# A share of the first score tiles transposed by TensorE instead of by DMA, under a newly drawn order

## The chip, the cores and the metric

One core of a Trainium2 chip runs the whole program in one launch. The metric is the device time of that core in microseconds (us). The kernel before takes 526.13 us, the median of three runs (523.61 to 528.75).

## The reference

Three layers follow each other, for a batch of 2 and 768 positions, all in float32 accuracy.

1. Attention with 8 heads of 64: `scores = scale * q k^T`, and a score counts only where the hashes of query and key agree (the hash is the sign of six projections). Then `softmax(scores) @ v`.
2. A mixture of four experts over the 512 channels that come out. Each expert is a causal attention with its own projections `wq, wk, wv, wo`; a gate picks the best two experts of each position and weighs them.
3. A mix with the previous position (`mu * x + (1 - mu) * x_prev`), then `sigmoid(xr @ w_r) * (relu(xk @ w_k)^2 @ w_v)`. The weights `w_k, w_v, w_r` arrive as 64-bit floats.

## The kernel before, in words

**Accuracy by halves.** Matmuls take 16-bit operands, so each value is split into a high part and a low part (`hi_part`, `lo_part`), and three matmuls (high by high, high by low, low by high) stand for one.

**Units.** The 2 x 768 positions are cut into twelve units of 128 queries. Each unit goes through `lsh_steps` (the hashed attention, 8 heads), `moe_steps` (4 experts) and `mix_steps`. Units overlap: while unit 1 is in its heads, unit 0 is in its experts.

**One score tile** (`softmax`, line 746, and `split_p`, line 764). TensorE (PE) writes the scores of 128 queries against n keys into PSUM (tile `s`; `se` for an expert). VectorE (DVE) copies them to `P` and takes the row minimum (`mx`); a small DVE instruction scales that. ScalarE (ACT) takes the exponential in place and the row sum. The high part goes to the first half of tile `PHL`, by GpSimd (POOL) for two tiles in eight and by ACT for the others; the low part goes to its second half, by POOL. `turn` (line 538) then transposes `PHL` to `PT`, 2n/128 blocks of 128 x 128, and `pv` multiplies `PT` by the values. For a head n is 768, so that there are twelve blocks; for an expert n grows from 128 in the first unit of a batch to 768 in its sixth, and the tiles are called `P_m`, `PHL_m`, `PT_m`.

**The transpose.** `turn` has two ways. With `by_pe` 0 the SyncE queue (SP) issues one DMA transpose. Otherwise PE transposes the blocks into PSUM, and they are copied out: for more than eight blocks into two PSUM tiles with one copy each, by ACT where `by_pe` is 3. The first operands' transposes (`tr_y`, `tr_x`) take this way already, with copies by DVE. For score tiles line 768 chooses, by `NS[0]`, the number of the score tile in the order in which the program is built (heads and experts of unit 0, then of unit 1, and so on). It takes the PE way where n is 768, `NS[0]` is under `pn`, and `NS[0] * pp % 8 < pp`. With `pn=0` no score tile does.

**Buffers.** There are two PSUM tiles for scores and four others (tag `d`) that nearly everything else shares: the head sums `x`, the projections, the transposes, the decoding of the 64-bit weights. `P` has four buffers, `PHL` six, `PT` three.

**Weights.** `split_w` (the experts' weights) and `split_d` (the 64-bit weights, 20 tiles) load a tile from the ACT queue, decode it by ACT, POOL and DVE, and split it. That is done during the first units.

**The order.** `plan` (line 220) draws up the order of all instructions on every engine ahead of time. Each step has a due time (`times`, line 1095, in units; `L`, `M`, `X`, `wa`, `k1` and the like move them), less a lead for what is urgent (`ev` for the copy of the scores, `ex` for the exponential, `hs`, `hp`, `ht`). At each point every engine looks at its first `win` ready steps and takes the one that can start first; a step may be up to `wait` ns later and still be taken for its rank. Engines execute in that order, each strictly one after the other; they wait for each other by semaphores.

Of the kernel before, what the change touches and what calls it, by code (L numbers as in the profile page):

```python
# [13 lines left out]
AF = mybir.ActivationFunctionType  # L14
OP = mybir.AluOpType
# [408 lines left out]
def tile_lsh_moe_mix(  # L424
# [8 lines left out]
    nc = Program(tc.nc)  # L433
# [12 lines left out]
    HS = S // 2  # L446
    NP, NPHL, NPT = CONF["np"], CONF["nphl"], CONF["npt"]

# [9 lines left out]
    def ahead(what, f, *a):  # L458

        old, nc.ahead = nc.ahead, nc.ahead + (what,)  # L460
        r = f(*a)
        nc.ahead = old
        return r
# [21 lines left out]
    def DQ():  # L485
        return QS[CONF["dq"]]

    def LQ(i):
        return QS[CONF["lq"]] if i else nc.sync

    def OQ():
        return QS[CONF["oq"]]

# [82 lines left out]
    def split_w(src_dmas, shape, dst, sc, nm):  # L576
        w32 = sp.tile(shape, F32, tag="x2t", bufs=CONF["nx2"], name=f"w32_{nm}")
        for dap, sap in src_dmas:
            DQ().dma_start(dap(w32), sap)
        hi, lo = dst(0), dst(1)  # L580
        if CONF["wd"]:
            nc.gpsimd.tensor_scalar(w32, w32, sc, 1.0, op0=OP.mult, op1=OP.mult)
            hi_part("a", hi, w32)
            lo_part("p", lo, w32, hi)
        else:
            hi_part("p", hi, w32, sc)
            lo_part("v", lo, w32, hi, sc)
# [158 lines left out]
    def softmax(Sv, n, scale, sm, bias, nm, masked=None):  # L746


        Pt = sp.tile([P, S], F32, tag="P", bufs=NP, name=f"P_{nm}")[:, :n]
        PHL = sp.tile([P, 2 * S], F16, tag="PHL", bufs=NPHL, name=f"PHL_{nm}")[:, :2 * n]  # L750
        PT = sp.tile([P, 2 * NT, P], F16, tag="PT", bufs=NPT, name=f"PT_{nm}")[:, :2 * n // P]
        dst = Pt.rearrange("p (a s) -> p a s", a=2) if len(Sv.shape) == 3 else Pt
        if masked:
            def evict():
                nc.vector.tensor_scalar(dst, Sv, masked, None, op0=OP.min, op1=OP.min, accum_out=bias)
                nc.vector.tensor_scalar(bias, bias, scale, None, op0=OP.mult)
        else:
            def evict():
                nc.vector.tensor_scalar(dst, Sv, -scale, None, op0=OP.mult, op1=OP.min, accum_out=bias)
        ahead("ev", evict)  # L760
        ahead("ex", lambda: nc.scalar.activation(Pt, Pt, AF.Exp, bias=bias, scale=-scale if masked else -1.0, accum_out=sm))
        return ahead("ht", split_p, Pt, PHL, PT, n)
# [9 lines left out]
    NS = [0]  # L772
# [4 lines left out]
    def lsh_steps(i, LAG):  # L777
# [3 lines left out]
        def score(h):  # L781
            need(KS[b, h // G][:3] + QS_[i])
            if t0 == 0 and h % 2:
                need(KS[b, h // 4])
            if h == 0:
                st["sm"] = sp.tile([P, H], F32, tag="sm", name=f"sm_{i}")
                st["mx"] = sp.tile([P, H], F32, tag="mx", name=f"mx_{i}")
            kg = KG[b, h // G]
            hh = h % G
            Sp = ps_s.tile([P, 2, 512], F32, tag="s", name=f"s_{i}_{h}")  # L790
            for n in range(2):
                for a, (x, y) in enumerate((("x1", "y1"), ("x2", "y2"))):
                    nc.tensor.matmul(Sp[:, n, :HS], QX[i][x][:, h, :], kg[y][:, hh, n * HS:(n + 1) * HS],
                                     start=(a == 0), stop=(a == 1))
            st["pt"][h] = softmax(Sp[:, :, :HS], S, -0.125 / (SQ * SK), st["sm"][:, h:h + 1],
                                  st["mx"][:, h:h + 1], f"{i}_{h}", MASKED)
# [41 lines left out]
    def moe_steps(i, LAG):  # L838
# [74 lines left out]
        def score(c):  # L913
# [27 lines left out]
            for r in range(2):  # L941
                e = 2 * c + r
                st["pt"][e] = softmax(Sv[r], n, 0.125 / (SMQ * SMQ), st["sm"][:, e:e + 1],
                                      sp.tile([P, 1], F32, tag="bias", bufs=4, name=f"bias_m{i}_{e}"), f"m{i}_{e}")
# [146 lines left out]
    L = [lsh_steps(i, CONF["lagl"]) for i in range(NU)]  # L1091
    M = [moe_steps(i, CONF["lagm"]) for i in range(NU)]
    X = [mix_steps(i) for i in range(NU)]
# [29 lines left out]
    with tc.manual_schedule():  # L1123
        nc.issue()


CONF = dict(L=[0.094, 0.041, 0.054, 0.082, 0.045, -0.033, 0.139, 0.173, 0.038, 0.077, 0.267, 0.124], M=[-0.049,
            -0.217, -0.048, 0.222, 0.058, 0.084, 0.136, -0.262, 0.269, 0.076, 0.421, -0.294], X=[-0.101, -0.04,
            -0.048, -0.037, 0.093, 0.282, 0.065, 0.021, 0.002, 0.125, -0.076, 0.316], ht=0.154, hf=-0.125, mq=0.03,
            mf=-0.045, wd=1, vd=0, wn=512, hd=0, pd=0, hl=8, hs=0.03, hp=0.044, ms=0.004, mp=0.085, k1=-2.858,  # L1130
            k1d=1.621, wa=0.047, wad=-1.27, wb=0.209, wbd=3.832, qo=0.987, ko=0.643, kg=0.23, kd=1.099, ld=-0.116,
            lagl=4, lagm=6, mo=1.227, md=1.497, xo=2.948, xd=1.219, np=4, nphl=6, npt=3, nx2=4, nf=5, dc=0, dq=2,
            lq=2, oq=2, ml='p', hg=2, ev=-0.037, ex=0.061, win=40, wait={'ACT': 0, 'POOL': 50, 'PE': 0, 'DVE': 0,
            'SP': 350}, te=0, kt=1, qt=12, pp=2, late=0.131, pn=0, pe=3, nraw=2, nmk=2, dm=500)

# [41 lines left out]
```

## Time and profile before

| | |
|---|---|
| median of three runs | 526.13 us |
| the profiled execution | 525.32 us, span of the instructions 523.5 us |
| PE busy | 443.3 us, 85% |
| DVE busy | 378.4 us, 72% |
| ACT busy | 349.1 us, 67% |
| POOL busy | 311.6 us, 60% |
| mean granted TensorE clock | 0.957 of full speed |

Times of rows are in us from the first instruction. A row of a group of instructions has the engine, the operation, the tile written and the tiles read, the shape, the count, the busy time, the mean of one in ns and the idle time ahead of them with what ended it. Every instruction stands under line 396, the helper that issues them, so that rows are told apart by tiles. "Issue" in the chain of waits is time in which the engine waited for nothing that the profile shows.

### The profile page before, as it was taken

The numbers are of one execution on the slowest core, as the hardware profiler recorded it, in microseconds if no ns is written. First come the engines' busy times: TensorE is split into PE (matmuls) and PEld (weight loads), VectorE is DVE, ScalarE is ACT, GpSimd is POOL, SyncE is SP. The second block draws the span as 40 slices with busy tenths as digits, with TensorE's granted clock in tenths as the row PEclk, the third lists the DMA queues.
The fourth block names the chain that finished last, engine by engine and source line by source line (L and its number), as shares of the span: only waits on it lengthen the run. The fifth ranks groups of instructions, "written<-read, shape, count | busy, mean of one in ns | idle before, by whom it ended". The sixth has DMA issues, their size and how long they took to land.

```text
span 523.5 us, 15721 instructions
## 1 busy us (share of the span) xinstructions
PE 443.3 (85%) x6288; PEld 335.6 (64%) x6288; DVE 378.4 (72%) x1094; ACT 349.1 (67%) x660; POOL 311.6 (60%) x286
## 2 busy tenths in 40 slices
PE   1666655486679899898898999998999999998997
PEld 1644454374466685685777678786786867876764
DVE  2789878688889958766987976866857687376432
ACT  3358855677777857956378977886665978558231
POOL 5879762755756934946464693962936568374110
PEclk9977879878899999999899999999999999999999
DMA  8749979599879996998479889496554889847200
GB/s 245 185 123 172 241 168 221 131 196 193 134 140 207 152 172 87 150 191 147 107 162 155 163 140 163 96 183 99 118 111 90 132 149 174 126 84 117 68 23 20
DMA packets 225243, 75.08 MB, mean 143 GB/s; under 512 B 216593, under 2 KB 220817, under 8 KB 225169
## 3 DMA queue, kind: packets, MB, share of 16 engines
q1 hardware_dynamic: 198288, 52.19, 60.0%
q10 hardware_dynamic: 26880, 21.88, 15.9%
q8 instruction: 49, 0.80, 0.6%
q14 instruction: 26, 0.20, 0.1%
HBM read 22.14 MB, written 3.15 MB: 48 GB/s over the span
## 4 chain that ended last, share of the span: by engine, by line
PE 40%; DMA 15%; DVE 13%; issue 9%; ACT 9%; POOL 7%; SPq 1%; ACTq 0%; POOLq 0%; DVEq 0%
DMA PT<-PHL 9%; PE h L396 8%; PE v L396 7%; PE s L396 5%; DMA PT_m<-PHL_m 5%; PE x L396 4%; PE r L396 4%; POOL PHL L396 3%; PE qk L396 3%; POOL PHL_m L396 2%; DVE P L396 2%; ACT P L396 2%; PE tr_x L396 2%; PE o L396 1%; DVE P_m L396 1%
## 5 line engine op out<-in xcount | busy, mean ns | idle before, releaser
L396 POOL TENSOR_TENSOR PHL<-P,PHL 128x768 f16<-128x768 f32 x96 | 159.1, 1667 | 56.2 <-ACT PHL L396 48.9
L396 DVE TENSOR_SCALAR_CACHE_REDUCE P<-s 128x768 f32<-128x768 f32 x96 | 91.1, 952 | 22.7 <-PE s L396 16.7
L396 ACT ACTIVATE P<-P,mx 128x768 f32<-128x768 f32 x96 | 89.1, 929 | 27.4 <-DVE mx L396 26.4
L396 PE MATMUL s<-y,x 128*128 128x384 f16 x384 | 81.7, 342 | 18.0 <-DVE P L396 13.4
L396 PE MATMUL x<-v,PT 128*128 128x64 f16 x1728 | 68.9, 197 | 11.4 <-DMA PT<-PHL 9.2
L396 PEld LDWEIGHTS <-PT 128*128 128x128 f16 x1728 | 63.6, 101 | 21.9 <-DMA PT<-PHL 12.7
L396 PE MATMUL h<-mk,WK 128*128 128x128 f16 x1152 | 74.7, 219 | 2.5 <-POOL mk L396 1.9
L396 PE MATMUL v<-WV,k 128*128 128x512 f16 x288 | 71.7, 379 | 0.7 <-DVE kT L396 0.7
L396 PEld LDWEIGHTS <-WK 128*128 128x128 f16 x1152 | 67.7, 98 | 7.0 <-issue 2.3
L396 PEld LDWEIGHTS <-x 128*128 128x128 f16 x576 | 42.0, 100 | 46.0 <-issue 24.9
L396 POOL TENSOR_TENSOR PHL_m<-P_m,PHL_m 128x128 f16<-128x128 f32 (+5 forms) x48 | 48.9, 1037 | 29.2 <-ACT PHL_m L396 28.6
L396 ACT ACTIVATE PHL<-P 128x768 f16<-128x768 f32 x72 | 59.8, 835 | 6.8 <-DMA PT_m<-PHL_m 4.1
L396 PE MATMUL qk<-xT,WQK 128*128 128x128 f16 x576 | 42.8, 229 | 3.6 <-DVE xT L396 1.9
L396 PEld LDWEIGHTS <-WQK 128*128 128x128 f16 x576 | 37.5, 103 | 6.8 <-issue 4.6
L396 PEld LDWEIGHTS <-k 128*128 128x128 f16 x288 | 26.1, 98 | 23.1 <-DVE kT L396 0.8
L396 ACT ACTIVATE P_m<-P_m,bias_m 128x128 f32<-128x128 f32 (+5 forms) x48 | 31.7, 660 | 11.2 <-DVE P_m L396 11.2
L396 PE MATMUL r<-WR,mr 128*128 128x512 f16 x144 | 36.6, 379 | 0.7 <-DVE e L396 0.7
L396 DVE TENSOR_SCALAR_CACHE_REDUCE P_m<-se 128x128 f32<-128x128 f32 (+5 forms) x48 | 28.6, 617 | 6.7 <-PE se L396 5.0
L396 ACT ACT_TABLE_LOAD x20 | 25.7, 1283 | 10.1 <-DMA consts<-in_consts_dram 7.1
L396 POOL TENSOR_TENSOR mr<-m32r,mr 128x512 f16<-128x512 f32 x12 | 13.9, 1159 | 30.4 <-ACT mr L396 30.4
L396 PE MATMUL y<-vn,PT_m 128*128 128x64 f16 x504 | 22.6, 195 | 8.5 <-DMA PT_m<-PHL_m 8.5
L396 PEld LDWEIGHTS <-PT_m 128*128 128x128 f16 x504 | 19.9, 99 | 14.7 <-DMA PT_m<-PHL_m 10.4
(127 smaller groups left out, 808.3 us busy)
## 6 DMA issues: line engine op xcount, KB each, us to landing
raw_k<-in_moe_w_k_dram ACTq DMA_DIRECT2D x8, 512.0 KB, 4.9
raw_v<-in_moe_w_v_dram ACTq DMA_DIRECT2D x8, 512.0 KB, 5.2
out_dram<-e ACTq DMA_DIRECT2D x12, 256.0 KB, 2.3
q<-in_q_dram ACTq DMA_DIRECT2D x11, 256.0 KB, 5.2
raw_r<-in_moe_w_r_dram ACTq DMA_DIRECT2D x4, 512.0 KB, 3.9
k<-in_k_dram SPq DMA_DIRECT2D x4, 384.0 KB, 6.0
v<-in_v_dram SPq DMA_DIRECT2D x4, 384.0 KB, 4.0
PT<-PHL SPq DMA_TRANSPOSE x96, 4.7
```

The lines of the kernel that those rows point to most:

```text
L396: getattr(getattr(self.nc, engine), method)(*[real(a) for a in args], **{k: real(a) for k, a in kw.items()})
```

## The change

`pn` goes from 0 to 32, which opens the PE way of line 768 for score tiles. Many due times and leads get new values, `win` goes from 40 to 80, and SP's `wait` from 350 to 300. `softmax` can let ACT scale the row minimum instead of DVE for tiles numbered under `bp`.

```diff
         if masked:
+            early = NS[0] < CONF["bp"]
+
             def evict():
                 nc.vector.tensor_scalar(dst, Sv, masked, None, op0=OP.min, op1=OP.min, accum_out=bias)
-                nc.vector.tensor_scalar(bias, bias, scale, None, op0=OP.mult)
+                if early:
+                    nc.scalar.activation(bias, bias, AF.Copy, scale=scale)
+                else:
+                    nc.vector.tensor_scalar(bias, bias, scale, None, op0=OP.mult)
...
-CONF = dict(L=[0.094, 0.041, 0.054, 0.082, 0.045, -0.033, 0.139, 0.173, 0.038, 0.077, 0.267, 0.124], M=[-0.049,
-            -0.217, -0.048, 0.222, 0.058, 0.084, 0.136, -0.262, 0.269, 0.076, 0.421, -0.294], X=[-0.101, -0.04,
-            -0.048, -0.037, 0.093, 0.282, 0.065, 0.021, 0.002, 0.125, -0.076, 0.316], ht=0.154, hf=-0.125, mq=0.03,
-            mf=-0.045, wd=1, vd=0, wn=512, hd=0, pd=0, hl=8, hs=0.03, hp=0.044, ms=0.004, mp=0.085, k1=-2.858,
-            k1d=1.621, wa=0.047, wad=-1.27, wb=0.209, wbd=3.832, qo=0.987, ko=0.643, kg=0.23, kd=1.099, ld=-0.116,
+CONF = dict(L=[0.343, 0.062, 0.124, 0.075, 0.047, -0.033, 0.139, 0.234, 0.03, 0.077, 0.258, 0.115], M=[-0.049,
+            -0.221, -0.018, 0.216, 0.057, 0.083, 0.137, -0.261, 0.237, 0.077, 0.422, -0.293], X=[-0.101, -0.04,
+            -0.048, 0.043, 0.098, 0.284, 0.07, 0.021, -0.007, 0.184, -0.064, 0.345], ht=0.154, hf=-0.122, mq=0.03,
+            mf=-0.043, wd=1, vd=0, wn=512, hd=0, pd=0, hl=8, hs=0.03, hp=0.044, ms=0.01, mp=0.087, k1=-2.713,
+            k1d=1.313, wa=-0.394, wad=-2.004, wb=0.209, wbd=3.832, qo=0.987, ko=0.643, kg=0.227, kd=1.101, ld=-0.116,
             lagl=4, lagm=6, mo=1.227, md=1.497, xo=2.948, xd=1.219, np=4, nphl=6, npt=3, nx2=4, nf=5, dc=0, dq=2,
-            lq=2, oq=2, ml='p', hg=2, ev=-0.037, ex=0.061, win=40, wait={'ACT': 0, 'POOL': 50, 'PE': 0, 'DVE': 0,
-            'SP': 350}, te=0, kt=1, qt=12, pp=2, late=0.131, pn=0, pe=3, nraw=2, nmk=2, dm=500)
+            lq=2, oq=2, ml='p', hg=2, ev=0.111, ex=0.096, win=80, wait={'ACT': 0, 'POOL': 50, 'PE': 0, 'DVE': 0,
+            'SP': 300}, te=0, kt=1, qt=12, pp=2, late=0.182, pn=32, pe=3, bp=0, nraw=2, nmk=2, dm=500)
```

## Rows read from the trace of the kernel before

**Rows 1.** Busy time by stretch: length, then each engine's busy us (instructions), clock, DMA share
```profile
core 0: us, PE busy (x) PEld busy (x) DVE busy (x) ACT busy (x) POOL busy (x), PEclk, DMA share, GB/s
0.00:36.00 36.00, 18.00 (x239) 14.63 (x240) 20.93 (x46) 13.03 (x19) 24.77 (x33) 0.91 0.73 194
36.00:72.00 36.00, 20.73 (x241) 13.89 (x239) 29.88 (x78) 31.53 (x58) 31.57 (x25) 0.82 0.93 195
72.00:102.00 30.00, 18.22 (x278) 14.63 (x278) 25.10 (x71) 13.65 (x34) 14.44 (x19) 0.90 0.74 172
102.00:135.00 33.00, 24.52 (x316) 18.78 (x316) 26.99 (x83) 25.17 (x53) 18.96 (x19) 0.81 0.99 185
135.00:280.00 145.00, 129.41 (x1960) 100.64 (x1959) 115.78 (x319) 100.84 (x183) 89.34 (x81) 0.98 0.86 150
280.00:500.00 220.00, 212.66 (x3089) 160.72 (x3086) 151.49 (x484) 159.43 (x309) 130.22 (x110) 1.00 0.73 125
```

**Rows 2.** Chain of waits, shares of the stretch 36 to 135 us
```profile
by line: issue 21.4%; POOL PHL L396 14.4%; DMA PT_m<-PHL_m 10.8%; ACT P L396 6.1%; DVE P L396 5.9%; DVE wd_k L396 5.6%; DVE wd_r L396 3.7%; ACT PHL L396 3.1%; DVE x L396 2.5%; POOL PHL_m L396 2.5%; DVE WK L396 2.3%; POOL wm_k L396 2.3%; DVE
```

**Rows 3.** Chain of waits, shares of the stretch 135 to 280 us
```profile
by line: DMA PT<-PHL 20.1%; PE h L396 6.5%; issue 6.0%; PE s L396 5.6%; PE x L396 5.1%; DMA raw_v<-in_moe_w_v_dram 4.9%; ACT L396 3.8%; DMA PT_m<-PHL_m 3.8%; PE tr_y L396 3.7%; DVE P L396 3.3%; PE r L396 3.2%; PE v L396 2.7%; ACT P L396 2.4
```

**Rows 4.** Tile PT, 36 to 72 us: issues (duration min/median/max), waiters, landing
```profile
L396 SPq DMA_TRANSPOSE PT<-PHL x11: 1419/1670/3467, 40.0 to 65.9; - x11
...
  PEld L396: 5.4, 3
  PE x L396: 4.3, 3
...
DMA to landing us min/median/max: 3.7/5.6/7.4
```

**Rows 5.** DMA queues of the whole span: packets, MB, share of 16 engines
```profile
q1 hardware_dynamic: 198288, 52.19, 60.0%
q10 hardware_dynamic: 26880, 21.88, 15.9%
```

**Rows 6.** SP queue's waits, 36 to 72 us: us, times, longest
```profile
SPq L396 <- POOL PHL L396: 10.0, 6, 2.7
SPq L396 <- PE x L396: 9.6, 4, 6.2
```

**Rows 7.** Tile tr_y, 17 to 22 us: transposes by PE, ns min/median/max of one
```profile
L396 PE MATMUL tr_y<-consts,nbk x24: 266/314/314, 18.0 to 20.4; 128*128 128x128 f16 x24
```

**Rows 8.** Timeline of PE: start, us, instructions; early and late in the span
```profile
18.03 2.72 PE L396 MATMUL tr_y<-consts,nbk 128*128 128x128 f16 x24 [0.83 <-DVE nbk L396]
...
252.82 2.31 PE L396 MATMUL tr_y<-consts,nbk 128*128 128x128 f16 x24 [1.38 <-DVE nbk L396]
```

**Rows 9.** Groups of ACT instructions, whole span: copies out of PSUM, and out of SBUF
```profile
L396 ACT ACTIVATE PHL<-P 128x768 f16<-128x768 f32 x72 | 59.8, 835 | 6.8 <-DMA PT_m<-PHL_m 4.1 <-DMA PT<-PHL 1.6 <-ACT P L396 0.3
...
L396 ACT ACTIVATE xT<-tr_x 128x512 f16<-128x512 f32 x12 | 7.0, 586 | 7.4 <-PE tr_x L396 7.3
...
L396 ACT ACTIVATE qT<-qk 128x256 f16<-128x256 f32 x12 | 4.5, 375 | 4.0 <-PE qk L396 3.9
```

**Rows 10.** What ACT waited for, 36 to 72 us: us, times, longest
```profile
ACT P L396 <- DVE mx L396: 5.9, 5, 2.3
```

**Rows 11.** What POOL waited for, 72 to 102 us: us, times, longest
```profile
POOL wm_k L396 <- ACT wm_k L396: 5.0, 1, 5.0
POOL PHL_m L396 <- ACT PHL_m L396: 4.9, 2, 4.6
POOL PHL_m L396 <- ACT P_m L396: 4.0, 1, 4.0
```

**Rows 12.** Groups of DVE instructions, 72 to 102 us: the work on weights
```profile
L396 DVE SCALAR_TENSOR_TENSOR wd_k<-raw_k,wd_k 128x512 uint32<-128x512 uint32 x8 | 5.5, 684 | 0.0
L396 DVE SCALAR_TENSOR_TENSOR WK<-wd_k,WK 128x512 f16<-128x512 f32 x4 | 2.7, 686 | 1.4 <-ACT WK L396 1.4
L396 DVE TENSOR_SCALAR wd_k<-wm_k 128x512 uint32<-128x512 uint32 x3 | 2.0, 683 | 0.0
```

## The prediction

> **What bounds the kernel now.** I read the busy time by stretch first, since a mean over the span mixes a crowded beginning with an end that belongs to PE. From 280 to 500 us PE is busy 212.7 of 220 us at its full clock: there nothing but less PE work helps, and the change takes none away. Subtracting PE's busy time from each stretch gives where its 80 us of idle time lie: 18.0 us up to 36, 15.3 from 36 to 72, 11.8 from 72 to 102, 8.5 from 102 to 135, 15.6 from 135 to 280, 7.3 from 280 to 500, and the rest behind [rows 1]. The span is PE's work plus this idle time, so a change of the beginning shows at the end only as far as it changes one of the two.
>
> The beginning has three faces [rows 1]. From 36 to 72 us nearly everything is full: DVE 29.9, ACT 31.5 and POOL 31.6 of 36 us, the DMA engines 0.93. From 72 to 102 there is a hole: ACT has 13.7 and POOL 14.4 of 30 us, while DVE still has 25.1. From 102 to 135 it is crowded again, DMA 0.99. The chain of waits says which of the full ones is the tight one from 36 to 135: POOL and DVE on `P` and `PHL`, ACT's exponentials, the decoding of weights on DVE (`wd_k`, `wd_r`), handovers ("issue"), and transposes of the experts' `PT_m`. The heads' `PT` is not among the terms that the row shows [rows 2]. It heads the chain only from 135 to 280, at 20.1% [rows 3], and the tiles that wait there are mostly ones the change leaves to DMA.
>
> **What is moved.** Line 768 wants a number under 32 that four divides, and n of 768. Unit 0 has numbers 0 to 11, unit 1 12 to 23, unit 2 24 to 35. The candidates are 0, 4, 8, 12, 16, 20, 24, 28; 8 and 20 are experts with 128 and 256 keys and keep the DMA. So six tiles move, heads 0 and 4 of units 0, 1 and 2. I put four of them into 36 to 72 and two into 102 to 135. `bp` is 0 and no number lies below it, so the new ACT scaling is never used.
>
> **DMA and SP lose six transposes.** In 36 to 72 each takes SP's queue 1.67 us (median) and lands after 5.6 us; PE stood 4.3 us for them before its matmuls, and 5.4 us before its weight loads, mostly the same time [rows 4]. The SP queue took 60.0% of 523.5 us, 314 us, for 52.19 MB [rows 5]; a head's tile is 128 x 1536 x 2 bytes, 0.393 MB, so 2.37 us of all sixteen engines. Six free 14.2 us, four of them 9.5 of the 33.5 us (0.93 x 36) that the DMA was busy in 36 to 72. Behind a moved transpose on SP stand only other transposes, and these stood waiting for POOL (10.0 us) or for a free `PT` (9.6 us) [rows 6], so the queue itself is not short of time. The gain lies between nothing and 9 us: PE's 4.3, and half of the chain's 10.8% of 99 us in `PT_m` [rows 2], were these small transposes to land faster on emptier engines. I take -1, since the chain hardly passes `PT`.
>
> **PE gains 72 transposes.** The like ones on `tr_y` last 266 to 314 ns from start to end [rows 7], but they overlap: 24 took 2.72 us early on (113 ns each) and 2.31 later (96 ns) [rows 8]. That is 8.2 us of work, 1.4 a tile, into 35.5 us of PE idle time between 36 and 135. PE takes its instructions in order: a transpose that stands ahead of POOL's low part holds back the scores and `x` behind it. The like wait was 0.83 and 1.38 us [rows 8], times six 5 to 8 us. I take +0.5, near the end of nothing, because PE is not the full engine there. [...]
>
> One figure of the Trainium skill speaks against the change: "VectorE: DVE Perf Modes", section "The three transpose paths", gives 390 ns for a 128 x 128 transpose on TensorE. By it the 72 would be 28 us of PE, an estimate, and the sum below would come out some 10 us later, with half of the surplus of 20 finding no idle PE. The trace does not agree: its rows have 96 to 113 ns, and the sum keeps to them.
>
> **ACT gains twelve copies.** None of this shape is in the trace. Out of PSUM, 256 columns took 375 ns and 512 took 586 [rows 9], 0.82 ns a column, so 768 cost 0.80 us; the copy of that length out of SBUF, 835 ns, is the upper neighbour. That is 1.6 us a tile, 9.6 in all: 6.4 into 36 to 72, where ACT then has 37.9 us to do in 36. Its only sizeable wait there was 5.9 us for the row minimum [rows 10]. Queued behind a copy that waits for PE are the exponentials and high parts of the next heads, and for those POOL waits. So 1.9 us must spill, into a stretch where ACT is idle more than half of the time; 3.2 us from 102 to 135 fit into 7.8 idle. Ends 0 and +9.6; I take +2, the overflow. The two PSUM tiles that a transpose takes, of four, are held for about 3 us (1.4 of PE, two copies). Were each time a step held up for one copy, that is +4.8; I take +0.5, since PE itself has time.
>
> **The order.** All else is due times. Unit 0's heads are due 0.25 of a unit later (a unit is about (500 - 36)/12 = 39 us, so 10 us), the experts' weights 0.44 earlier and more, copies of scores get 0.15 of a unit more lead, and twice as many steps are looked at. The trace has no row for that; the hole bounds it. In 72 to 102 POOL stood 13.9 us in three waits for ACT [rows 11], ACT was idle for 16, and DVE did 10.2 us of weight decoding [rows 12] that unit 0's later rank lets come sooner. What DVE has idle from 36 to 135 is 99 - 82.0 = 17 us [rows 1], and without taking work off DVE no order shortens the stretch by more; 12 is my end for a gain. The end for a loss is +8: unit 0's ten us of lateness handed on to its experts almost whole. I take -5.5, near half of the hole's 11.8 us of PE idle, because an order that has ACT at 0.88 in one stretch and at 0.46 in the next has room.
>
> **Sum.** -1 + 0.5 + 2 + 0.5 - 5.5 = -3.5 on the profiled execution's 525.3 us; the median stands 0.8 above it, so 526.1 - 3.5 = 522.6 us.
>
> **Rivals.**
> *The hole closes.* If moving ACT's and DVE's work out of the crowd lets the order take 11 of its 12, DMA gives 3 and ACT costs 2, the time is 514. For it speaks that all engines but DVE idle in the hole; against, that DVE has only 4.9 us of idle time there.
> *ACT becomes the bound.* From 36 to 72 ACT is the second fullest engine before it gets anything. If its load there passes 36 us and the order moves nothing else away, all twelve copies (9.6) lie on the path, POOL's `PHL` behind them; with 1 from DMA and 2 from the order this is +6.6, or 533. Against it: the idle ACT right behind.
> *Slow transposes.* Each as long as its longest record, without overlap: 72 x 0.314 = 22.6 us of PE, 14 over my term, of which some 8 find no idle time: 534. The timeline's rows speak against it. The 390 ns of the Trainium skill would be this case.
> *Hidden anyway.* The transposes were off the path, DVE's work is the same, the order trades one wait for another: 526.
>
> **How the numbers follow.** Chances: forecast 0.32 (its own range 518 to 527), the hole 0.32, ACT 0.20, hidden 0.13, slow transposes 0.03. A change under 1% (5.3 us) can hardly be told from none here. Faster by more: 0.32 and an eighth of the forecast's chance, 0.36; slower: 0.20 + 0.03 = 0.23; within: 0.41. The range reaches from below the hole's 514 to just above ACT's 533, 511 to 534, with about one in ten left out at each end.
>
> **What would show it.** Right: 90 transposes of `PT` on SP instead of 96; ACT copies near 0.80 us; 72 more PE instructions near 0.1 us apart; the stretch around 72 to 102 with less PE idle time than 11.8 us. Wrong: ACT above 0.95 busy from 36 to 72 with POOL's wait for `PHL` grown (the ACT case); PE idle before 135 unchanged from 53.5 us (hidden); or idle time that comes back after 135, where `PT` heads the chain, because what is early there has nothing to feed.

## The result and the profile after

The changed kernel takes 529.45 us (median of 20 runs, 526.69 to 534.04); the kernel before, on the same chip, 526.98 us (20 runs). The ratio is 1.0065, 95% interval 1.0044 to 1.0086: slower by 3.4 us (2.3 to 4.5). The two medians are 2.5 us apart. Ratios, here and below, are taken over undisturbed runs and medians over all, so that the two can part by some 0.3%, in e5 by more. The change is within the 1% that the prediction called hard to tell from none, and on the wrong side of its 522.6 us; the range, 511 to 534, holds it. The profiled execution took 530.35 us, span 528.5.

The changed kernel's busy time by stretch, columns as in [rows 1]:

```profile
0.00:36.00 36.00, 16.70 (x229) 14.76 (x230) 18.82 (x39) 12.45 (x18) 24.49 (x33) 0.87 0.73 194
36.00:72.00 36.00, 25.10 (x272) 16.14 (x271) 31.16 (x77) 30.78 (x55) 27.20 (x22) 0.80 0.65 133
72.00:102.00 30.00, 20.65 (x274) 16.49 (x273) 22.54 (x69) 18.18 (x41) 14.43 (x18) 0.77 0.81 172
102.00:135.00 33.00, 25.58 (x344) 20.17 (x344) 29.32 (x81) 26.86 (x55) 21.51 (x21) 0.84 0.68 137
135.00:280.00 145.00, 126.88 (x1887) 96.94 (x1888) 115.56 (x325) 99.22 (x184) 89.80 (x81) 0.96 0.80 152
280.00:500.00 220.00, 213.78 (x3130) 162.09 (x3127) 152.43 (x488) 163.00 (x311) 133.17 (x113) 1.00 0.77 131
```

Subtract PE's busy time from each length, as was done for before. PE is now idle 10.9, 9.4 and 7.4 us in the three stretches from 36 to 135, 27.7 in all against 35.5: the middle did get tighter, and ACT's hole filled (18.2 us against 13.7). But up to 36 us PE is idle 19.3 against 18.0, from 135 to 280 it is 18.1 against 15.6, and PE's busy time over the span rose from 443.3 to 452.9 us. So the span's +5.0 us is PE's +9.6 less 4.6 of idle time. The transposes themselves are 6.3 of the 9.6; the other 3.3 are the same instructions as before, which took longer in this execution, with a granted clock of 0.945 on the mean against 0.957. In 72 to 102 the row has 0.77 where [rows 1] has 0.90. In a second profiled execution of the changed kernel (e16, below) the tighter middle is there again (29.6 us idle), and so is a longer busy time, 451.0 us; but PE is idle only 18.3 us up to 36 and 14.7 from 135 to 280, so what this one execution gave back at the two ends is not steady. The chain of waits of this execution can be followed back only to 475 us, so [rows 2, 3] have no answer here.

The moved tiles in the changed kernel: first their instructions over the whole span (duration ns min/median/max), then PE's and ACT's busy time on them from 36 to 72, 72 to 102 and 102 to 135 us:

```profile
L396 PE MATMUL tr_PT<-consts,PHL x72: 216/219/314, 40.4 to 113.3; 128*128 128x128 f16 x72
L396 ACT COPY PT<-tr_PT x12: 772/791/817, 41.2 to 120.4; 128x768 f16<-128x768 f16 x12
```

```profile
36.00:72.00 36.00, 3.19 (x36) 4.32 (x6) 0.80 0.65 133
72.00:102.00 30.00, 1.00 (x12) 1.70 (x3) 0.77 0.81 172
102.00:135.00 33.00, 2.08 (x24) 3.08 (x4) 0.84 0.68 137
```

PE's busy times add to 6.27 us for 72 transposes: 87 ns of PE's time each, though one lasts 219 from start to end. Three tiles fell into 36 to 72, not four.

What DMA still does for `PT` from 36 to 72 us, the whole span's two large queues, and what ACT (36 to 72) and POOL (72 to 102) waited for in the changed kernel:

```profile
L396 SPq DMA_TRANSPOSE PT<-PHL x8: 1419/1556/3814, 45.1 to 71.0; - x8
...
  PE x L396: 3.5, 2
```

```profile
q1 hardware_dynamic: 188880, 49.83, 56.8%
q10 hardware_dynamic: 26880, 21.88, 15.0%
```

```profile
ACT P L396 <- DVE mx L396: 8.0, 6, 4.5
```

```profile
POOL nbq L396 <- PE tr_x L396: 7.9, 1, 7.9
POOL PHL L396 <- DMA PT<-PHL: 4.0, 1, 4.0
```

Against [rows 4, 5] there are eight transposes by DMA instead of eleven, PE stands 3.5 us for them instead of 4.3, and SP's queue moves 2.36 MB less, six tiles of 0.393. ACT's wait for the row minimum grew from 5.9 to 8.0 us [rows 10]. Of POOL's three waits of [rows 11], 13.9 us in all, 3.1 are left, but it is as idle in the hole as before (14.4 us busy in both): a new wait of 7.9 us, for PE to transpose the next unit's queries, took their place.

### The profile page after: what moved, and what is told of

It is laid out like the page before. It is cut to its first block, busy times and chain, and to the rows that moved or that the text cites. A ratio compares the mean times of both kernels' runs of the same rounds, so it can differ in the third digit from the quotient of the medians.

```text
span 528.5 us, 15851 instructions
## 1 busy us (share of the span) xinstructions
PE 452.9 (86%) x6360; PEld 342.3 (65%) x6360; DVE 379.5 (72%) x1094; ACT 357.4 (68%) x672; POOL 312.9 (59%) x286
## 5 line engine op out<-in xcount | busy, mean ns | idle before, releaser
L396 PE MATMUL s<-y,x 128*128 128x384 f16 x384 | 83.4, 349 | 9.0 <-DVE P L396 7.1
L396 PE MATMUL x<-v,PT 128*128 128x64 f16 x1728 | 67.4, 196 | 13.9 <-DMA PT<-PHL 12.5
L396 PEld LDWEIGHTS <-PT 128*128 128x128 f16 x1728 | 62.1, 100 | 23.3 <-DMA PT<-PHL 15.3
L396 PE MATMUL h<-mk,WK 128*128 128x128 f16 x1152 | 76.6, 221 | 0.3 <-DVE x L396 0.2
L396 PEld LDWEIGHTS <-WK 128*128 128x128 f16 x1152 | 69.2, 99 | 4.9 <-issue 0.9
L396 POOL TENSOR_SCALAR PHL<-P 128x768 f16<-128x768 f32 x24 | 20.7, 867 | 19.2 <-ACT P L396 12.4
L396 POOL TENSOR_TENSOR mr<-m32r,mr 128x512 f16<-128x512 f32 x12 | 14.5, 1208 | 27.8 <-ACT mr L396 27.7
L396 DVE SCALAR_TENSOR_TENSOR h<-h,t 128x512 f32<-128x512 f32 x24 | 16.7, 697 | 16.2 <-ACT t L396 16.1
```

The costliest lines, as they stand in the source:

```text
L396: getattr(getattr(self.nc, engine), method)(*[real(a) for a in args], **{k: real(a) for k, a in kw.items()})
```

## The experiments

Three things changed at once: six tiles moved; the order of the first 30 us; the order of all that follows. The experiments swap them one at a time. "In place" means that the drawn order is kept, instruction by instruction, and only the tiles' own instructions are exchanged. Ratios are to the kernel before on the same chip, with 95% intervals; 0.1% is 0.53 us. In kernels with an inserted line the helper that issues the instructions stands at line 397 instead of 396.

**e1, new times without the tiles.** The changed kernel with the new due times, drawn up anew, and all score tiles by DMA.

```diff
-            'SP': 300}, te=0, kt=1, qt=12, pp=2, late=0.182, pn=32, pe=3, bp=0, nraw=2, nmk=2, dm=500)
+            'SP': 300}, te=0, kt=1, qt=12, pp=2, late=0.182, pn=0, pe=3, bp=0, nraw=2, nmk=2, dm=500)
```

> The new due times, leads and win, but no score tile by TensorE (pn back to 0); the order is drawn up from them afresh. If the new order is what costs (theory A), this is slower than before by as much as the change, 528 to 531. If the moved transposes cost (theory B: ACT's 9 us of copies and PE's 6 us in the crowded beginning), it is 525 to 527. If each redrawn order simply lands somewhere (theory C), anything from 523 to 531.

530.7 us, 1.0056 (1.0017 to 1.0096). The due times, which I had put at -5.5 us, gain nothing by themselves.

**e2, old times with the tiles.** The kernel before with `pn=32`, drawn up anew.

> The old due times with pn 32, the order drawn up afresh around the six moved tiles. Theory A: as before, 526 to 528. Theory B: as after or worse, 529 to 533, since nothing was adapted to them. Theory C: anything from 523 to 533.

542.47 us, 1.0322 (1.0274 to 1.0369). The old due times with six longer steps in them make a much worse order, worse than any of the three ranges: it is the pairing of tiles and order that counts.

**e3, the changed kernel's order with the tiles by DMA.** In place: at the second transpose's position stands a DMA transpose, and the other three instructions are empty.

```diff
+    for PT, PHL, k, made in SWAP:
+        pe0, act0, pe1, act1 = made
+        pe1.calls = [("sync", "dma_start_transpose", (PT, PHL), {})]
+        for o in (pe0, act0, act1):
+            o.calls = []
```

> Exactly the order of the changed kernel, instruction by instruction, only that each of the six tiles is transposed by one DMA at the place where PE's second half stood, and the copies are gone. Theory A: still 528 to 531. Theory B: 523 to 526, below before, because PE loses 6 us and ACT 9.

548.76 us, 1.0402 (1.0346 to 1.0458): 3.4% above the changed kernel and far above both ranges. Two of e3's longest waits for `PT`, 36 to 200 us (us, times, longest):

```profile
PE x L396 <- DMA PT<-PHL: 18.5, 9, 3.7
...
ACT PHL_m L396 <- DMA PT<-PHL: 9.5, 4, 4.4
```

In the changed kernel the first is 9.5 us and the second is not among its longest. The new order is drawn for tiles that arrive soon; with DMA the tiles of 36 to 72 us land after 5.7 us (median), and PE, which takes its instructions in turn, stands before the head sums. Not all of the loss is waiting. Between the two profiled executions the span grows by 19.8 us (528.5 to 548.3): PE is idle for 17.3 us more, and busy for 2.5 more (455.4 against 452.9) although 6.3 us of transposes are gone. The same instructions thus took 8.8 us longer, with a mean granted clock of 0.925 against 0.945.

**e4, the kernel before with the tiles moved in place.** The DMA transpose is replaced by the two groups of transposes on PE, and the two copies go into ACT's order 1.0 and 1.9 us of planned time behind.

```diff
+        (dma,) = made
...
+        turn(PT, PHL, f"PT_{k}", 3)
+        pe0, act0, pe1, act1 = nc.ops
+        i = nc.order.index(dma)
...
+        nc.order[i:i + 1] = [pe0, pe1]
...
+        for o, d in ((act0, LATER[0]), (act1, LATER[1])):
```

> Exactly the order of the kernel before, only that the six DMA transposes are replaced where they stand by 12 PE transposes each and two ACT copies set in about 1.0 and 1.9 us behind. Theory A: 526 to 528. Theory B: 529 to 534. No order is redrawn here, so theory C has no say.

529.0 us, 1.0057 (1.0024 to 1.0089). The move alone, without any new order, costs 3.0 us (1.3 to 4.7) by the ratio and 1.8 by the medians, for this one placement of the copies; -1, +0.5, +2 and +0.5 had made +2.

**e5 and e6, the two halves of e4.** e5 keeps the DMA and adds the 72 transposes on PE, into PSUM that nobody reads. e6 keeps the DMA and adds twelve copies of 128 x 768 on ACT, from `PHL` to a spare tile.

```diff
+            for c in range(6):
+                nc.tensor.transpose(pt[:, c * P:(c + 1) * P], PHL[:, (j * 6 + c) * P:(j * 6 + c + 1) * P], ident16)
...
+        nc.order[i + 1:i + 1] = [pe0, pe1]
```
```diff
+            nc.scalar.copy(dump, PHL[:, j * S:(j + 1) * S])
...
+            nc.order.insert(q, act)
```

> The order of the kernel before with its DMA transposes all kept; beside the six of them PE does the 72 transposes of the change as well, into PSUM tiles that nobody reads. It prices PE's share alone. If PE's 6 us of new work is what shows (theory PE, since PE is busy 97% of the later half and any work put on it comes out at the end), 529 to 531, near the in-place version with copies (529.0, +0.6%). If ACT's copies were the cost (theory ACT), 526.5 to 527.5.

> The order of the kernel before with its DMA transposes all kept; beside them ACT makes the 12 copies of 768 columns, here from the halves of PHL into a spare tile, at the places where the in-place version had them. It prices ACT's 9 to 10 us alone. Theory ACT: 529 to 531. Theory PE: 526.5 to 528.

e5: 526.69 us against 526.87 for before, so PE's 72 instructions cost nothing that shows. (Its ratio, 0.9915, is the one that parts most from the medians, its fastest run being a single one of 518.1 us; the means of all runs differ by -1.1 us, +-2.0.) e6: 529.37 us, 1.0075 (1.0043 to 1.0107): the copies alone cost as much as the whole move. Without the kernel before in between, e6 is 3.1 us (+-2.0) slower than e5 on the same chip, by the means of twelve runs each. Three rows of 36 to 135 us, of e4, e5 and e6 (columns as in [rows 1]); then, of e6 alone, its copies (busy us, mean ns, idle time ahead) and its chain of waits over the same stretch:

```profile
36.00:135.00 99.00, 68.08 (x892) 53.58 (x890) 79.57 (x223) 75.03 (x148) 61.18 (x58) 0.84 0.72 152
```
```profile
36.00:135.00 99.00, 66.92 (x910) 51.37 (x908) 82.10 (x232) 71.04 (x144) 65.35 (x61) 0.87 0.92 184
```
```profile
36.00:135.00 99.00, 61.31 (x817) 45.65 (x815) 78.50 (x220) 76.48 (x150) 63.36 (x60) 0.85 0.91 183
```
```profile
L397 ACT COPY dump<-PHL 128x768 f16<-128x768 f16 x12 | 9.9, 822 | 0.1
```
```profile
by line: issue 19.9%; POOL PHL L397 14.1%; DMA PT_m<-PHL_m 11.4%; ACT P L397 6.4%; ACT dump L397 4.6%; DVE wd_k L397 4.1%; DVE P L397 3.9%; DVE wd_r L397 3.1%; POOL wm_k L397 2.9%; ACT PHL L397 2.8%; PE tr_x L397 2.6%; ACT P_m L397 2.5%; PO
```

In e5 PE has 66.9 of 99 us to do instead of 63.5: room enough. In e6 DVE and POOL do 3.5 and 1.6 us less of their work in these 99 us than the 82.0 and 65.0 that add up in [rows 1] (up to 36 us they had done 1.3 and 0.5 us more), and the copies stand in the chain with 4.6% of 99 us, 4.6 us. The execution profiled is e6's fastest, 525.14 us, so its rows show where the copies stand and not what they cost. In e4 the DMA share fell from 0.89 to 0.72 and gave nothing that can be measured: e4 less e6 is -0.2% (+-0.5).

**e9 and e10, the copies by DVE.** In e4's order (e9) and in the changed kernel's exact order (e10).

```diff
-        turn(PT, PHL, f"PT_{k}", 3)
+        turn(PT, PHL, f"PT_{k}", 1)
```
```diff
+            o.calls = [("vector", "tensor_copy", args, kw)]
```

> The order of the kernel before, the six DMA transposes replaced in place by PE's, and the copies made by DVE (0.55 us each, 6.6 in all) instead of ACT, at the same places. PE's work alone cost nothing and ACT's copies alone as much as the whole. If it is ACT's crowd that costs, this is 525 to 527.5; if any engine of the crowded beginning pays for 6 to 9 us more, 528.5 to 531.

> The changed kernel's order exactly, only that each copy out of PSUM is made by DVE at the place where ACT made it. If the copies on ACT cost in the new order as in the old, 526 to 528; if the new order was drawn around them and its loss is its own, 529 to 532.

e9: 530.82 us, 1.0055 (1.0019 to 1.0092). e10: 530.25 us, 1.0071 (1.0035 to 1.0108). DVE copies a half in 551 ns (e9) instead of 791, and nothing is gained: it costs as much on either engine of the crowded beginning.

**e11, four later tiles.** In place as e4, but the tiles numbered 36, 42, 60 and 67, which are transposed between 135 and 243 us, where `PT` heads the chain [rows 3].

```diff
-        if n == S and NS[0] < 32 and NS[0] % 4 == 0:
+        if NS[0] in (36, 42, 60, 67):
```

> The order of the kernel before, four other heads' tiles (numbers 36, 42, 60, 67: the first and the seventh of unit 3, the first and the eighth of unit 5; three of them stood on the chain of waits between 135 and 245 us) transposed by PE in place with ACT copies, the first 32 all left to DMA. If the waits for PT there can be bought off, 522 to 525; if PE, busy 89% of that stretch, or ACT pays as much as the waits gave, 526.5 to 529.

531.56 us, 1.0092 (1.006 to 1.0125), above both ranges: four tiles cost 4.9 us there, more than six at the beginning. A transfer at the head of the chain was not replaced by something cheaper; why it came out so dear was not followed.

**e8 and e12, the kernel before drawn up anew for a trifle.** `hs` from 0.03 to 0.031 (e8), `kg` from 0.23 to 0.231 (e12).

> The kernel before, no tile by TensorE, with one lead moved by a hair (hs 0.030 to 0.031, 0.04 us in due time), so that the order is drawn up afresh. If a redrawn order lands anywhere near (theory C), it is off by 1 to 5 us in either direction, 522 to 532; if the time follows the due times smoothly, 526.5 to 527.5.

> The kernel before, no tile by TensorE, one spacing of the due times moved by a hair (kg 0.230 to 0.231); some 40% of PE's instructions change places. If a redrawn order costs by itself because the old one was the pick of many, 528 to 531 again; if it scatters both ways, 523 to 531.

e8: 529.39 us, 1.0045 (1.0008 to 1.0082). e12: 525.95 us, 0.9995 (0.9956 to 1.0034). In these two draws a new order costs between nothing and half a per cent without any reason in the due times, so most of e1's 0.56% needs no other.

**e7, e15 and e17, the changed kernel with the old start.** The order of what is planned before 30 us is taken from the old times, the rest stays. e15 takes that start from the new times with the old `wa` and `wad` (the experts' weights) alone. It comes out as the same program, so those two values make the whole difference of the start. e16 is the changed kernel again, beside e17 on one chip.

```diff
+    HALF = dict(CONF, wa=OLD["wa"], wad=OLD["wad"])
+    nc.times(HALF)
+    nc.plan(HALF)
+    first = []
+    for o in nc.order:
+        if o.step_at >= START:
+            break
+        first.append(o)
+    nc.times(CONF)
...
+    nc.order = first + [o for o in nc.order if o not in done]
```

> The changed kernel, six tiles by TensorE, whose first 30 us are put in the order that the old due times give (the first scores stood at 31.7 us before, at 34.5 after), all the rest in the changed kernel's order. If the late start is what the new order costs, 526 to 527.5, back by the 2 to 3 us. If the start is made up for by what follows, 529 to 531 as the change.

> The changed kernel, six tiles by TensorE, whose first 30 us are drawn up from the new due times but with the old ones of the experts' weights (wa 0.047, wad -1.27). If these two numbers make the late start, the first scores stand at 31 to 33 us and the time is 526.5 to 528.5; if not, scores at 34 to 35 us and 529 to 531.

> The changed kernel with the old order of the first 30 us (the program of e7 and e15 once more). By the theory that the late start costs the changed kernel its loss: 0.997 to 1.003 (525.5 to 528.5 us), and below e16's on the same chip. By the rival that e7 and e15 came out low by chance: as e16, 1.004 to 1.009.

> The changed kernel once more, for comparison with the two kernels sent beside it: by every theory what it gave before, 1.004 to 1.009 of the kernel before (529 to 531.5 us), first score tiles at 34.5 us.

e7: 528.08 us, 1.0025 (0.9991 to 1.006). e15: 526.61, 0.9986 (0.9961 to 1.0011). e17: 526.48, 1.0024 (0.9986 to 1.0061). e16: 529.49, 1.0083 (1.005 to 1.0115). Weighted by the inverse square of their half widths, the three with the old start make 1.0005 (+-0.0018), the two with the new start 1.0070 (+-0.0018): the start costs 0.65% (+-0.25), 3.4 us, nearly all that the changed kernel loses. The means of all runs give 2.6 us, again the whole of the loss that they show, and e16 against e17 on one chip 2.1 us (+-1.7). e7 by itself fell between its two ranges.

The trace shows what is late in it. PE from 18 us to the first scores, in the changed kernel and then in e15 (start, us, instructions):

```profile
18.98 2.72 PE L396 MATMUL tr_y<-consts,nbk 128*128 128x128 f16 x24 [0.83 <-POOL w_v L396]
...
25.20 0.62 PE L396 MATMUL tr_x<-consts,naq 128*128 128x128 f16 x8 [1.38 <-DVE naq L396]
...
28.91 2.72 PE L396 MATMUL tr_y<-consts,nbk 128*128 128x128 f16 x24 [1.89 <-POOL w_qk L396]
...
34.46 1.78 PE L396 MATMUL s<-y,x 128*128 128x384 f16 x5 [0.85 <-DVE x L396]
```
```profile
17.96 2.72 PE L397 MATMUL tr_y<-consts,nbk 128*128 128x128 f16 x24 [0.84 <-DVE nbk L397]
...
23.28 0.61 PE L397 MATMUL tr_x<-consts,naq 128*128 128x128 f16 x8
...
26.89 1.62 PE L397 MATMUL tr_y<-consts,nbk 128*128 128x128 f16 x24 [1.76 <-DVE nbk L397]
...
31.62 3.76 PE L397 MATMUL s<-y,x 128*128 128x384 f16 x12 [0.85 <-DVE x L397]
```

The lag is 1.0 us at the first row, 1.9 at the queries' transposes, 2.0 at the next ones and 2.8 at the scores. The first us is not the order's: ACT's first instruction waits for the constants (`consts`), which landed at another time in each execution. Here it is in the changed kernel, in e15 and in e16, with e16's first scores behind (34.5 had been expected):

```profile
7.27 1.28 ACT L396 ACT_TABLE_LOAD   x1 [7.27 <-DMA consts<-in_consts_dram]
```
```profile
6.19 1.28 ACT L397 ACT_TABLE_LOAD   x1 [6.19 <-DMA consts<-in_consts_dram]
```
```profile
6.54 1.28 ACT L396 ACT_TABLE_LOAD   x1 [6.54 <-DMA consts<-in_consts_dram]
...
33.50 2.74 PE L396 MATMUL s<-y,x 128*128 128x384 f16 x8 [0.85 <-DVE x L396]
```

In e7 and e17 the first scores stand at 32.22 and 32.68, so that the changed kernel's are 1.8 us later on the mean of its two executions and the three with the old start. DVE shows where the second us of the pair comes from, again first the changed kernel, then e15:

```profile
19.82 4.73 DVE L396 COPY y<-tr_y 128x768 f16<-128x768 f16 x8 [0.98 <-PE tr_y L396]
24.46 0.68 DVE L396 SCALAR_TENSOR_TENSOR naq<-q,naq 128x512 f16<-128x512 f32 x1
```
```profile
18.80 1.84 DVE L397 COPY y<-tr_y 128x768 f16<-128x768 f16 x3 [0.98 <-PE tr_y L397]
21.61 0.69 DVE L397 SCALAR_TENSOR_TENSOR naq<-q,naq 128x512 f16<-128x512 f32 x1 [0.97 <-ACT naq L397]
22.22 2.41 DVE L397 COPY y<-tr_y 128x768 f16<-128x768 f16 x5
```

The queries' low part (`naq`), which PE's next transposes need, stands behind eight copies in the new order and behind three in the old one. In e16, whose eight copies start at 18.80 us just as e15's three do, it starts at 23.48 instead of 21.61, and the scores come 1.9 us later. That the earlier weights pushed it back in the plan follows from the two values that e15 exchanged; no row shows it. Single profiled executions don't show the difference at the end reliably (spans 528.5 and 524.9 us for the changed kernel, 526.3, 523.4 and 528.9 for the old start): the verdict is that of the ratios, the trace only shows what is late. The runs show, then, that the order of the first 30 us costs this; that it does so because the first scores come late is argued, and 1.8 us of lateness would have to cost about 3 at the end.

**e13, e14 and e18, the start elsewhere.** e13: the new start before the old rest, no tile moved. e14: the old start before the new rest, no tile moved. e18: e13 with the six tiles moved in place as in e4.

```diff
+    nc.times(CONF)
+    first = []
+    for o in nc.order:
+        if o.step_at >= START:
+            break
+        first.append(o)
+    nc.times(OLD)
+    nc.plan(OLD)
```

> No tile by TensorE. The first 30 us in the order of the new due times, all the rest in the order of the old ones. If the new start is the part of the new order that costs (theory start), 528.5 to 530; if it is the rest of the new order, 526 to 527.5.

> No tile by TensorE. The first 30 us in the order of the old due times, all the rest in the order of the new ones: the run with new due times and DMA (530.7, +0.56%) with its start undone. Theory start: 526.5 to 528. If the rest costs: 529 to 531.

> The kernel before with six tiles moved to TensorE and ScalarE in place (e4), and its first 30 us in the changed kernel's order. By the theory that a late start costs wherever tiles go by TensorE: e4's 0.6% and some 0.3 to 0.7% more, 1.009 to 1.013 (531.5 to 534 us), first scores near 34.5 us. By the rival that the start costs only within the newly drawn order: 1.002 to 1.009, as e4.

e13: 528.08 us, 1.0019 (0.9989 to 1.005), with its first scores at 34.58 us. This lies between its two ranges. e14: 530.48 us, 1.0064 (1.0012 to 1.0116), no better than e1, against what the theory of the start had forecast. e18: 531.14 us, 1.0121 (1.0066 to 1.0177), 0.6% above e4 (+-0.65), as expected by the theory of the start, though by itself this does not exclude none. With the tiles on DMA the new start shows no cost that can be told from noise (0.19%, +-0.31, in e13, whose first scores are as late as the changed kernel's); with the tiles on PE it costs 0.65% under the new order, and perhaps the same under the old one. That it depends on the tiles is suggested by this and not shown, and why it would stays open. That the DMA engines, 0.89 and 0.90 busy from 36 to 135 in before and e13 but 0.71 in the changed kernel, are there the tighter limit without the move and swallow 2.5 us is only an argument.

No version was shown to beat the kernel before; e5, e7, e12, e13, e15 and e17 can't be told from it.

## Why the prediction was wrong

**The step that failed is the order, -5.5 us.** It took the hole as a bound and a half of it as the gain. Two things were lumped in it, and the runs part them. Going from e4 (old start, old rest, tiles moved) to the three runs with the old start and the new rest changes the ratio from 1.0057 to 1.0005: -2.7 us (+-1.9). Going on to the new start adds 3.4 us (+-1.3). So the rest of the order gained half of what I put, and the start gave it all back: taken whole, from e4 to the changed kernel, the order is worth +0.7 us (+-1.9) instead of -5.5. The tiles' own terms, +2 in the sum and 3.0 in e4, account for only about 1 us of the miss. I had the cause in hand: "the experts' weights 0.44 earlier and more" stands in my list of due times, and I read it only as relief for the hole, not as something that could put the first queries' own steps later. Lateness stood in my working only as the end for a loss, +8, and from the due time of unit 0's heads; e15, whose start is drawn with that new due time, shows none of it there. The stretch up to 36 us, 18.0 us of PE idle time in my own reading of [rows 1], the largest of all, got no term. The reading that fails in general is that an order "has room": e1, e8 and e12 show three orders drawn afresh that moved this kernel by 0 to 0.6%, none to the fast side.

**The hole** closed as the rival had it, for ACT (13.7 to 18.2 us) and by 2.4 us of PE's idle time, but POOL's idle time there stayed under another name. And PE's idle time was a bad sign: of the 7.9 us less from 36 to 135, 6.3 are the new transposes, which fill idle time without anything coming earlier. In e4, whose order is the old one, PE already has only 8.7 us idle from 72 to 102 (the row has 21.34 of 30 us busy), no more than the changed kernel's 9.4 and 8.6 (e16).

```profile
72.00:102.00 30.00, 21.34 (x286) 17.50 (x285) 22.49 (x67) 16.08 (x36) 12.11 (x17) 0.79 0.68 150
```

**The clock** has no term in the sum, and the runs ask for none that they can size. The granted clock, a mix of 1.2 and 2.4 GHz, is 0.952 on the mean of all 145 runs of the kernel before that the experiments recorded (0.942 to 0.964), 0.955 in e4's runs and 0.953 in e5's, which have the transposes in the old order, 0.948 and 0.951 in the changed kernel's, and 0.952 to 0.955 with the old start. So the transposes left it, and the orders differ by less than the runs of one kernel; only e1 and e14 (0.941 and 0.942), e2 (0.942) and e3 (0.931) lie lower. For the same instructions PE was busy 452.9 and 451.0 us in the changed kernel's two profiled executions and 452.9, 450.6 and 452.3 in the three with the old start: the start's loss is not seen as a slower PE. From 22 to 34 us, where PE waits longer for the late operands, the granted clock tends to be lower with the new start, 0.65 to 0.73 in six profiled executions against 0.63 to 0.84 in ten with the old one; what that costs the runs don't separate from the late operands.

**DMA, -1:** not contradicted. e4 against e6, which differ by the DMA and PE's part, gives -0.9 us (+-2.4), an interval that also holds zero, though the DMA share fell by 0.17 of 99 us, 17 us of engine time. That freeing the DMA buys little is as the working had it.

**PE, +0.5:** not contradicted; e5 shows no cost (-1.1 us, +-2.0), and PE stood 0.5 us for POOL's low part ahead of the transposes, where the upper end had 5 to 8. The 72 transposes are 87 ns apart where I had 96 to 113. The rival of slow transposes is out; the 390 ns of the Trainium skill ("VectorE: DVE Perf Modes", section "The three transpose paths") is not seen: one takes 219 ns here from start to end, and 87 of PE's time where they follow each other.

**ACT, +2, and PSUM, +0.5:** right in kind, probably too small. The copies last 0.79 us (0.80 forecast), but twelve of them cost 3.9 us (2.3 to 5.6) in e6, twice what I took as overflow (2.5 by the medians), and e4 as a whole 3.0. The overflow is hardly the measure: the copies stand ahead of exponentials and high parts in ACT's order, and in e6's rows DVE and POOL get less done around them. That DVE's shorter copies cost the same (e9) speaks for a chain that is held up and not for one engine's sum; the runs don't show which chain. For PSUM the changed kernel's trace has one wait, of 2.0 us, in which a transpose stood until a copy had freed its tile.

**ACT as the bound:** not as stated. ACT had 30.8 of 36 us, not above 0.95, because the new order moved other work off 36 to 72 (without the copies ACT has 26.5 us there, 31.5 before) and three tiles went there, not four. Its result (533) was near the truth (529.45) for another reason.

**Hidden anyway (526):** its clue, PE idle before 135 unchanged from 53.5 us, did not show (47.0), and the move was not free (e4). The result is nearer to 526 than to the forecast all the same.

**The signs I named:** 90 transposes left on SP, 72 more on PE, 0.79 us copies and less than 11.8 us of idle time in the hole all came true, and the kernel was slower. They were signs that the parts do what they should, not that the sum holds. Of those for the wrong side, idle time that comes back after 135 did in the first profiled execution, 18.1 us against 15.6, but not in e16's, 14.7.

## What to carry to other kernels

A change of due times is first to be read for what it puts ahead of the very first operands: find the instruction that the bounding engine waits for before its first real work, and look whether anything now stands ahead of it on the engines that feed it. To price a move inside a planned order, make the move in place and the new order separately: here, with the tiles moved, the new order's start and its rest had opposite signs, and neither could be seen in the sum. A hole in an engine's busy time bounds a gain and doesn't estimate it, and it shrinks also when only more work is put into it. A lag read from one pair of profiled executions wants a second pair: here 1 us of 2.8 was the time at which one of the first transfers landed.

## What was not expected of the hardware

The same order of instructions lost 3.4% when six transposes of 0.393 MB went back to DMA (e3's ratio 1.0402 against 1.0065), about 18 us for six transfers, where transfers land after some 5.7 us: in an order drawn for early operands a late one cost far more than its own time, part of it as waits and part as a lower granted clock (0.925 against 0.945). In the order drawn for DMA the same exchange was worth 0.6% in DMA's favour (e4). And a DMA share lowered from 0.89 to 0.72 over 99 us, in the fullest stretch of the kernel, bought nothing that the runs can show.
